# Infini-attention block: probabilities from a second, turned score product instead of transposes; row sums of the last head group on TensorE

## The chip, the cores and the metric

One core of a Trainium2 chip. The metric is the device time of one execution in microseconds (us), the median of several runs. The engines that matter here: TensorE (PE, with its weight loads PEld), VectorE (DVE), ScalarE (ACT), GpSimd (POOL), and SyncE (SP), whose queue issues nearly all DMAs.

## The reference

One pre-LayerNorm block on x of 1 x 2048 x 1024: an attention with a compressive memory, and then a channel MLP. There are H = 32 heads of width 32 and N = 4 segments of L = 512 rows. Cut to what matters:

```python
logits = einsum("bhqd,bhkd->bhqk", qs, ks) * scale + mask   # causal inside a segment, 512 x 512
p = softmax(logits)
a_dot = einsum("bhqk,bhkd->bhqd", p, vs)
pq = phi(qs)                                  # phi(t) = t + 1 if t > 0 else exp(t)
a_mem = (pq @ M) / (pq @ z + 1e-6)            # memory of the segments before
o = g * a_mem + (1 - g) * a_dot               # g = sigmoid(beta), one number a head
M, z = M + phi(ks).T @ vs, z + phi(ks).sum(0)
...
h = x + o @ wo
out = h + gelu(layernorm(h) @ w1 + b1) @ w2 + b2     # 1024 -> 3584 -> 1024
```

## The kernel before, in words

**Halves, groups, units.** The sequence is done in two halves of two segments. In each half the 32 heads are taken in eight groups `g` of four heads. A unit is one group in one segment: 2 x 8 x 2 = 32 units. After the 16 units of a half comes the product with `wo` (tile `pwo`); the MLP fills the rest of the span.

**Precision.** Each dense fp32 product is made of three fp32r products of high and low parts: `yh*wh`, `yl*wh`, `yh*wl`, the helper at L128, L129 and L130. A unit has 24 slots of such a triple (three projections `kps`, `qps`, `vps` of eight chunks of 128 rows), each matmul 128x512.

**Scores.** Query and key of a head are put on top of each other as high and low parts, so that one matmul with 96 rows makes the three partial products: `ks` has (high, low, high), `qs` (high, high, low). These stacks are written by DMA: `ks` goes through DRAM (`stack`, L410 and L412), `qs` for three heads from SBUF to SBUF (L407) and for one head through DRAM.

**The attention of a unit** runs one unit late, among the 24 slots of the next. `slot` has six steps for a head, and the table `HEAD` says at which step each operation of which pipeline stage is issued. For each head: four score matmuls `pqk` (L594, widths 128, 384, 256, 512, since a row block only needs the keys up to its diagonal); for each a DVE reduction (L595) that adds the mask, scales with minus, writes `pr` in SBUF and leaves the row minimum (minus the maximum) in `mx`; an ACT exponential (L603) with the row sum as its accumulator; ten PE transposes of 128x128 (`ppt`, L642, in groups of 4, 4 and 2); their copies to SBUF, one by DVE (L645, 512 wide) and two by ACT (L647, 512 and 256). After the four heads of a unit: the product with the values (`po`, L437, sixteen matmuls with 32 columns of weights, followed by the sixteen small `pmm` of the memory update); reciprocals of the sums (L610), times 1 - g on POOL (L613), transposed on PE (`pw`, L623), stored to `r_dram` (L626) and read back spread over 32 rows a head (L628); the scaling of `po` (L667) and the memory part (L670).

**Order.** PE keeps the program's order through the units. After the last unit's dense slots the order is free: there the scheduler mixes what is left of the attention with the matmuls of `pwo`. `TIMES` holds the slots of the unit's other operations (when keys and queries are evacuated, when a turned tile goes through `turn_dram` and back, when `o` is stored). SP issues its DMAs strictly in program order, and one that waits holds up those behind it.

**Banks.** PSUM: three banks for dense products, two `qk` for the scores, two `pt` for the transposes, one `av` for `po`. Weight casts `wh` of k and v are on ACT and that of q on DVE (L718), the low parts on POOL (L720).

## Time and profile before

| what | value |
|---|---|
| median of 3 runs | 2197.75 us (2196.99 to 2205.3) |
| the profiled execution | 2198.85 us |
| its span | 2197.1 us |
| granted TensorE clock over the span | 0.998 |
| PE busy | 2166.8 us (99%) |
| DVE busy | 1334.3 us (61%) |
| ACT busy | 1029.8 us (47%) |
| POOL busy | 740.2 us (34%) |
| DMA | 437.39 MB, mean 199 GB/s |

Busy times overlap one another. For PE the page models the ends of matmuls, and matmuls overlap in it, so a busy share of 99% says that PE is hardly ever empty, not that it works at its peak. What an instruction costs PE is read from the distance between two starts, in the timeline. The chain of waits follows the work that ended last back through whatever released it, and gives the share of the span by line.

### The profile page before, as it was taken

The numbers are of one execution on the slowest core, as the hardware profiler recorded it, in microseconds if no ns is written. First come the engines' busy times: TensorE is split into PE (matmuls) and PEld (weight loads), VectorE is DVE, ScalarE is ACT, GpSimd is POOL, SyncE is SP. The second block draws the span as 40 slices with busy tenths as digits, with TensorE's granted clock in tenths as the row PEclk, the third lists the DMA queues.
The fourth block names the chain that finished last, engine by engine and source line by source line (L and its number), as shares of the span: only waits on it lengthen the run. The fifth ranks groups of instructions, "written<-read, shape, count | busy, mean of one in ns | idle before, by whom it ended". The sixth has DMA issues, their size and how long they took to land.

```text
span 2197.1 us, 34393 instructions
## 1 busy us (share of the span) xinstructions
PE 2166.8 (99%) x11865; PEld 1758.3 (80%) x11865; DVE 1334.3 (61%) x2689; ACT 1029.8 (47%) x2219; POOL 740.2 (34%) x584
## 2 busy tenths in 40 slices
PE   8999999999999999999999999999999999999999
PEld 6788887868888887888888768888888788888887
DVE  6666665666745665666666656745666665576563
ACT  6566665653643445666666653543343222322321
POOL 4122221233434432122222233444445644155340
PEclk9999999999999999999999999999999999999999
DMA  7676666765575556666666755575659865576772
GB/s 229 187 198 183 192 195 196 201 200 201 173 215 163 172 160 192 184 193 188 196 191 185 202 178 197 159 211 157 182 177 375 290 229 192 180 248 219 243 240 91
DMA packets 400792, 437.39 MB, mean 199 GB/s; under 512 B 33102, under 2 KB 267114, under 8 KB 400618
## 3 DMA queue, kind: packets, MB, share of 16 engines
q1 hardware_dynamic: 337450, 398.48, 59.2%
q10 hardware_dynamic: 63168, 36.71, 5.6%
q8 instruction: 94, 1.54, 0.3%
q14 instruction: 80, 0.66, 0.1%
HBM read 287.41 MB, written 128.78 MB: 189 GB/s over the span
## 4 chain that ended last, share of the span: by engine, by line
PE 88%; DMA 3%; POOL 3%; ACT 2%; DVE 1%; issue 1%; SPq 1%; POOLq 0%; ACTq 0%
PE po L1376 21%; PE bps L980 10%; PE cps L980 7%; PE dps L980 7%; PE ppt L642 6%; PE pqk L594 4%; PE po L437 3%; PE qps L128 3%; PE kps L128 3%; PE vps L128 3%; PE kps L129 3%; PE kps L130 3%; PE qps L130 3%; PE qps L129 3%; PE vps L129 2%; PE vps L130 2%
## 5 line engine op out<-in xcount | busy, mean ns | idle before, releaser
L603 ACT ACTIVATE pr<-pr,mx 128x128 f32<-128x128 f32 (+3 forms) x512 | 287.0, 561 | 237.2 <-DVE mx L595 236.5
L595 DVE CUSTOM_DVE_ANT_0 pr<-pqk,mask 128x128 f32<-128x128 f32 (+3 forms) x512 | 241.3, 483 | 129.0 <-PE pqk L594 123.3
L642 PE MATMUL ppt<-ident,pr 128*128 128x128 f32 x1280 | 215.8, 273 | 5.1 <-ACT pr L603 2.3
L642 PEld LDWEIGHTS ppt<-ident,pr 128*128 128x128 f32 x1280 | 163.6, 140 | 54.5 <-DVE pt L645 3.7
L1386 DVE TENSOR_TENSOR c<-c,po 128x512 f32<-128x512 f32 x160 | 105.4, 683 | 138.9 <-PE po L1376 131.9
L594 PE MATMUL pqk<-ks,qs 96*128 96x128 f32 (+3 forms) x512 | 182.9, 359 | 2.9 <-DMA qs<-ql 1.8
L720 POOL TENSOR_TENSOR wl<-wr,wh 128x1024 fp32r<-128x1024 f32 x42 | 105.7, 2517 | 144.5 <-ACT wh L718 131.5
L647 ACT COPY pt<-ppt 128x512 f32<-128x512 f32 (+1 forms) x256 | 119.6, 468 | 55.9 <-PE po L437 38.9
L645 DVE COPY pt<-ppt 128x512 f32<-128x512 f32 x128 | 88.1, 689 | 70.3 <-PE ppt L642 59.3
L1376 PE MATMUL po<-w2h,zh 128*128 128x512 f32 x378 | 121.0, 390 | 1.4 <-ACT zh L1315 1.0
L594 PEld LDWEIGHTS pqk<-ks,qs 96*128 96x128 f32 x512 | 96.7, 189 | 21.8 <-issue 6.1
L980 PE MATMUL bps<-zh,sb 128*128 128x512 f32 x336 | 111.0, 391 | 0.0
L980 PE MATMUL bps<-zh,sa 128*128 128x512 f32 x336 | 110.8, 390 | 0.0
L128 PE MATMUL kps<-yh,wh 128*128 128x512 f32 (+1 forms) x264 | 110.0, 417 | 0.0
L1233 POOL TENSOR_TENSOR w2r<-w2r 128x512 f32<-128x512 f32 x54 | 84.0, 1565 | 71.2 <-DMA w2r<-in_B_w 68.6
L128 PE MATMUL qps<-yh,wh 128*128 128x512 f32 x256 | 107.4, 419 | 0.0
L128 PE MATMUL vps<-yh,wh 128*128 128x512 f32 x256 | 106.1, 414 | 0.0
L1376 PE MATMUL po<-w2h,hl 128*128 128x512 f32 x322 | 103.3, 390 | 0.2
L130 PE MATMUL kps<-yh,wl 128*128 128x512 f32 (+1 forms) x264 | 103.2, 391 | 0.0
L129 PE MATMUL kps<-yl,wh 128*128 128x512 f32 (+1 forms) x264 | 102.9, 390 | 0.1
L130 PE MATMUL vps<-yh,wl 128*128 128x512 f32 x256 | 100.8, 394 | 0.0
L130 PE MATMUL qps<-yh,wl 128*128 128x512 f32 x256 | 100.7, 394 | 0.0
(245 smaller groups left out, 5792.4 us busy)
## 6 DMA issues: line engine op xcount, KB each, us to landing
hr<-h_dram SPq DMA_DIRECT2D x112, 448.0 KB, 5.2
w2r<-in_B_w SPq DMA_DIRECT2D x122, 256.0 KB, 4.4
r<-in_B_w SPq DMA_DIRECT2D x56, 512.0 KB, 4.5
ks<-ks_dram SPq DMA_DIRECT2D x128, 192.0 KB, 3.5
h_dram<-ht ACTq DMA_DIRECT2D x84, 256.0 KB, 3.8
ks_dram<-kh SPq DMA_DIRECT2D x64, 256.0 KB, 2.7
wr<-in_A_wo SPq DMA_DIRECT2D x32, 512.0 KB, 4.6
wx<-in_B_w SPq DMA_DIRECT2D x56, 256.0 KB, 3.4
```

The lines of the kernel that those rows point to most:

```text
L128: nc.tensor.matmul(ps, ah, bh, start=first, stop=False)
L129: nc.tensor.matmul(ps, ah, bl, start=False, stop=False)
L130: acts["mm"] = nc.tensor.matmul(ps, al, bh, start=False, stop=last)
L594: nc.tensor.matmul(pqk[:, :n], u["qs"][j][:, i * P:(i + 1) * P], u["ks"][j][:, 0:n], start=True, stop=True)
L595: nc.vector.tensor_tensor_reduce(out=st["pr"][:, offs[i]:offs[i] + n], in0=pqk[:, :n], in1=mask[:, 512 - n:512], op0=ALU.add, op1=ALU.min, ...
L603: nc.scalar.activation(pi, pi, AF.Exp, bias=mx[:, i:i + 1], scale=-1.0, accum_out=mx[:, 4 + i:5 + i])
L642: nc.tensor.transpose(ppt[:, o:o + P], pr[:, offs[i] + jk * P:offs[i] + (jk + 1) * P], ident)
L647: nc.scalar.copy(pt, ppt[:, :w])
L720: nc.gpsimd.tensor_tensor(wl[:, c:c + WLC], wr[:, c:c + WLC], raw(wh)[:, c:c + WLC], op=ALU.subtract)
L980: nc.tensor.matmul(ps, x_[:, c, :], y_[:, c, :], start=first and c == 0 and n == 0, stop=last and c == 3 and n == 2, skip_group_check=True)
L1376: nc.tensor.matmul(ps, x_[:, k], y_[k], start=opens and k == 0 and i == 0, stop=closes and k == self.KP - 1 and i == 2, skip_group_check=True)
L1386: nc.vector.tensor_tensor(o, o, ps, op=ALU.subtract if name == "4" else ALU.add)
```

## The change

The probabilities are needed with the keys on the partitions, for the product with the values. Before, they were made with the queries on the partitions and turned on PE. Now a second score product makes them turned: `again` multiplies the stacks with their roles exchanged (`ks` as weights, `qs` as data; tile `psc`), and ACT's exponential of it is the tile that the value product reads. The row maximum has to be subtracted there along the columns, which is done in the product itself: the stacks have 98 rows, `ks` with 1.0 in the two more rows, and `qs` with minus the row maximum as a high and a low part.

```diff
-TIMES = dict(pk=10, kx=12, ks=11, qs=16, pq=16, omt=34, vx=24, pm=25, pmm=30, pmf=40, om=35, od=67, ...
+TIMES = dict(pk=12, kx=15, ks=9, kf=21, qs=17, qf=22, pq=18, omt=42, vx=24, pm=27, pmm=30, pmf=37, om=43, od=89, ...
+FOLLOW = dict(q=28.2, x=47.3, y=47.4, z=50.2, r=47.6, w=51.2, p=60.3, a=82.3, o=85.2)
+PACE = dict(q=(4.7,1.2), p=(4.0, 1.3))
...
+        def fetch(name, n, p):
+            nc.sync.dma_start(raw(stacks[name][n][0:96, 2 * p:2 * p + 2]),
+                              s_dram[name][n][64 * p:64 * p + 64].rearrange("(j r) b n -> (r b) j n", j=2))
...
+            for p in range(2):
+                at(T["kf"] + 7 * p, partial(stack_fetch, "ks", p))
+                at(T["qf"] + 6.5 * p, partial(stack_fetch, "qs", p))
...
+        def qk(u, j, i):
...
+            pqk = psum.tile([P, 512], F32, tag="qk", name="pqk", bufs=4)
...
+            nc.vector.tensor_tensor_reduce(out=pqk[:, :n], in0=pqk[:, :n], in1=mask[:, 512 - n:512], op0=ALU.add, op1=ALU.min,
+                                           scale=-1.0, scalar=3.0e38, accum_out=mx[:, k:k + 1])
+            if u["g"] < NG - 1:
+                nc.scalar.activation(pqk[:, :n], pqk[:, :n], AF.Exp, bias=mx[:, k:k + 1], scale=-1.0, accum_out=mx[:, 16 + k:17 + k])
...
+        def rows_in(u):
+            d = m_dram[u["md"]].rearrange("(a c k) r -> c k a r", a=4, c=2)
+            for c in range(2):
+                BQ.dma_start(raw(u["qs"][96 + c:97 + c]).rearrange("p j (i a r) -> p (j i) a r", i=4, a=4), d[c])
+
+        def again(u, j, n):
+            w = sum(P * (4 - jk) for jk in groups[n])
+            pt = ab.tile([P, w], F32, name=f"pt{n}", bufs=4)
+            ps = psum.tile([P, 512], F32, tag="qk", name="psc", bufs=4)
...
+                nc.tensor.matmul(ps[:, o:o + m], u["ks"][:, j, jk * P:(jk + 1) * P], u["qs"][:, j, P * jk:], start=True, stop=True)
...
+            nc.scalar.activation(pt, ps[:, :w], AF.Exp)
...
+            nc.gpsimd.affine_select(d, d, pattern=[[1, P]] if len(groups[n]) == 1 else [[0, 2], [1, P]],
+                                    compare_op=ALU.is_ge, fill=0.0, base=0, channel_multiplier=-1)
...
-            nc.vector.reciprocal(rs[:, 4 * j:4 * j + 4], st["mx"][:, 4:8])
...
+            if u["g"] == NG - 1:
+                den = psum.tile([P, 512], F32, tag="qk", name="den", bufs=4)
+                abreast([(den[32 * j:32 * j + 32, 0:P], ones, u["pt", 0][j][:, 0:P], True, True) for j in range(4)])
+                abreast([(den[32 * j:32 * j + 32, P:], ones, u["sm"][j], True, True) for j in range(4)])
+                nc.vector.reciprocal(u["w"], den)
```

What goes with it:

- **The first product stays**, with its reduction, but both now work in place in PSUM: its exponential is only for the row sums (`mx`), and nothing of it is copied out. Scores and second scores share one ring of four banks (`qk`), where there were two rings of two.
- **The maximum's way**: per unit a copy, a difference and a 32x32 block transpose of the 16 maxima of a row on DVE (`largest`), one store to `m_dram` (slot 47.4) and two loads of 1x64x32 into rows 96 and 97 of `qs` (slot 50.2). The second products begin at slot 60.3.
- **The mask** of the second product is an `affine_select` on POOL on each of the diagonal blocks after the exponential, three a head.
- **Stacks**: each unit stores three blocks of each stack to DRAM and fetches two heads at a time, 96x2x512. None of the stacks goes from SBUF to SBUF any more. The return of a turned tile from `turn_dram` (`back`) is issued three slots after its store (`HOP`).
- **The last group of a half** (`g == 7`, two units a half, four in all) makes no row sums on ACT. DVE adds the turned probabilities into `sm` (three additions a head), eight fp32 matmuls with ones make the sums already spread as `po` is (`den`), a reciprocal of 128x512 on DVE inverts them, and one more instruction (L721 of the new kernel) scales `po`. The way over `pw` and `r_dram` is left out there.
- **Scale and casts**: the scale is folded into the evacuation of the queries. The weight casts of k and v go from ACT to DVE, so that all three are there.
- **Time**: the attention of a unit now reaches from slot 28 to slot 85 after its unit's start, so that it spans two following units; `HEAD` and `slot` are gone, and every operation has its slot in `FOLLOW` or `LAST_FOLLOW` and its distance between heads in `PACE` or `LAST_PACE`.

The line numbers of the new kernel differ from those of the profile before. On PE, in the `vps` slots of a unit in the middle of a half, the program before had this for one head (`yh`, `yl`: the input's parts; `wh`, `wl`: the weights'):

```order
L594 MATMUL pqk<-ks,qs 128x128
L128 MATMUL vps<-yh_204,wh 128x512
L129 MATMUL vps<-yl_205,wh 128x512
L130 MATMUL vps<-yh_204,wl 128x512
L642 MATMUL ppt<-ident,pr 128x128 x4
L594 MATMUL pqk<-ks,qs 128x384
```

In the changed program the same place, the `vps` slots of a unit, reads:

```order
L664 MATMUL psc<-qs_374,ks_372 128x512
L632 MATMUL pqk<-ks_373,qs_375 128x256
L135 MATMUL vps<-yh_439,wh 128x512
L136 MATMUL vps<-yl_440,wh 128x512
L137 MATMUL vps<-yh_439,wl 128x512
L664 MATMUL psc<-qs_374,ks_372 128x384
L664 MATMUL psc<-qs_374,ks_372 128x128
L632 MATMUL pqk<-ks_373,qs_375 128x512
```

Where a group of four transposes stood beside a score matmul, one or two matmuls of the second product of the unit before (`ks_372`, `qs_374`) stand beside a score matmul of the current one (`ks_373`, `qs_375`).

On SP, around the point where the inverse sums of a unit go out to `r_dram`, before (`qs_dram`, `ks_dram`: stacks; `turn_dram`: a turned tile; `wr`: a weight):

```order
L412 DMA qs<-qs_dram_166 96x512
L374 DMA sch<-turn_dram_159 32x4x128 x4
L626 DMA r_dram_161<-sch 16x128
L410 DMA ks_dram_163<-kh 128x512
L410 DMA ks_dram_163<-kl 128x512
L410 DMA ks_dram_163<-kh 128x512
L628 DMA sch<-r_dram_161 32x512 x4
```

The same point in the changed program:

```order
L648 DMA m_dram_169<-mt 128x32
L381 DMA turn_dram_160<-sch 128x512
L697 DMA r_dram_163<-sch 16x128
L420 DMA ks_373<-ks_dram_166 96x2x512
L653 DMA qs_374<-m_dram_169 1x64x32 x2
L386 DMA sch<-turn_dram_160 32x4x128 x4
L699 DMA sch<-r_dram_163 32x512 x4
L420 DMA qs_375<-qs_dram_168 96x2x512
```

The fetch of the second half of the next unit's query stack (the last row) stands behind the store and the reload of the inverse sums, behind the two loads of the maxima and behind the return of a turned tile. Before, the query stack had been issued ahead of the store.

On DVE, after the dense slots of a half have ended, with the first of the two last units at its end (`sm`, `den`: the sums of the last group):

```order
L678 TENSOR_TENSOR sm<-sm,pt_5560 128x256
L547 TENSOR_TENSOR MZ<-pmm,MZ 128x128
L634 ISA pqk,mx<-pqk,mask 128x128
L634 ISA mx 128x1
L711 RECIPROCAL scl<-den 128x512
L634 ISA pqk,mx<-pqk,mask 128x384
```

Before, the scaling of `po` in that place stood with a copy of a transposed tile and with no reciprocal of that size:

```order
L610 RECIPROCAL rs<-mx 128x4
L645 COPY pt_6249<-ppt 128x512
L529 TENSOR_TENSOR MZ<-pmm,MZ 128x128
L667 TENSOR_TENSOR scl<-po,scl 128x512
L104 TENSOR_TENSOR ol_5550<-scl,oh_5549 128x512
```

The wide reciprocal and the additions of `sm` have come in between the reductions of the very last unit and the scaling of `po`.

More of the change, by code (lines that the diff above doesn't have):

```diff
@@ L96, in build @@
     s_dram = {n: [dram.tile([P, 3, 512], F32, name=f"{n}_dram{k}") for k in range(2)] for n in ("ks", "qs")}
+    m_dram = [dram.tile([P, 32], F32, name=f"m_dram{k}") for k in range(2)]
     acts = {}
@@ L372, in turned, with back @@
             TQ.dma_start(d, mid)
+            return d
+        def back(d, to):
             for c in range(4):
@@ L545, in memory_turn @@
                     one_small()
-                turned(v["om"], u["omt"], tmp("omx"))
+                d = turned(v["om"], tmp("omx"))
+                at(T["om"] + HOP, lambda: back(d, u["omt"]))
             if g < NG - 1:
@@ L1045, in c1 @@
                 if j < HP:
-                    ps = self.banks[j] = bank("cps", ("qk", "pt")[j % 2], 2)
+                    ps = self.banks[j] = bank("cps", "qk", 4)
                     h, l, _ = left[j - 2]
@@ L1128, in pair @@
             self.made(j + 1, "S2", "S1")
-            dps = bank("dps", "pt", 2)
+            dps = bank("dps", "qk", 4)
             if j < HP - 1:
```

265 lines of the change are left out of this document (130 added, 135 removed).

## The prediction

> **What bounds the kernel now.** First the page's busy times and its chain of waits:
>
> ```profile
> PE 2166.8 (99%) x11865; PEld 1758.3 (80%) x11865; DVE 1334.3 (61%) x2689; ACT 1029.8 (47%) x2219; POOL 740.2 (34%) x584
> PE 88%; DMA 3%; POOL 3%; ACT 2%; DVE 1%; issue 1%; SPq 1%; POOLq 0%; ACTq 0%
> by line: PE po L1376 21.2%; PE bps L980 10.3%; PE cps L980 7.0%; PE dps L980 6.8%; PE ppt L642 5.8%; PE pqk L594 3.6%; PE po L437 2.9%; PE qps L128 2.7%; PE kps L128 2.6%; PE vps L128 2.6%; PE kps L129 2.5%; PE kps L130 2.5%; PE qps L130 2.
> ```
>
> The end is set by PE for 88% of the span. The transposes `ppt` hold 5.8% of it, 0.058 x 2197.1 = 127.4 us, or 127.4 / 128 = 1.0 us for each of the 128 heads in segments; the four score matmuls hold 3.6%, 79.1 us, 0.62 us a head. Then four windows of 27 us: two with dense slots and attention in the two halves, and the two tails, where the last units meet the product with `wo`. Columns after the window: span, then the busy time of PE, PEld, DVE, ACT, POOL, then clock, DMA share and GB/s.
>
> ```profile
> 404.00:431.00 27.00, 27.00 (x198) 21.63 (x196) 16.63 (x52) 16.52 (x47) 1.88 (x5) 1.00 0.65 191
> 1037.00:1064.00 27.00, 27.00 (x170) 21.60 (x169) 17.65 (x56) 17.00 (x48) 7.00 (x5) 1.00 0.52 152
> 458.00:485.00 27.00, 24.75 (x144) 18.69 (x143) 17.24 (x34) 13.53 (x33) 8.10 (x7) 1.00 0.61 201
> 1289.00:1316.00 27.00, 25.86 (x134) 17.98 (x133) 14.80 (x24) 10.71 (x23) 11.86 (x9) 1.00 0.59 177
> ```
>
> In the first two PE never idles at clock 1.00, and DVE and ACT have some 10 us free: there a microsecond off PE's queue is a microsecond off the time, as long as nobody makes PE wait. The tails are looser already: PE is empty for 27.00 - 24.75 = 2.25 and 27.00 - 25.86 = 1.14 us. Last, PE's timeline over one head (start, duration; durations overlap, so I use starts):
>
> ```profile
> 405.83 0.23 PE L594 MATMUL pqk<-ks,qs 96*128 96x128 f32 x1
> ...
> 406.63 0.60 PE L642 MATMUL ppt<-ident,pr 128*128 128x128 f32 x4
> 406.98 0.44 PE L594 MATMUL pqk<-ks,qs 96*128 96x384 f32 x1
> ...
> 407.95 0.28 PE L594 MATMUL pqk<-ks,qs 96*128 96x256 f32 x1
> ...
> 408.77 0.60 PE L642 MATMUL ppt<-ident,pr 128*128 128x128 f32 x4
> 409.12 0.48 PE L594 MATMUL pqk<-ks,qs 96*128 96x512 f32 x1
> ...
> 410.14 0.38 PE L642 MATMUL ppt<-ident,pr 128*128 128x128 f32 x2
> 410.27 0.48 PE L128 MATMUL vps<-yh,wh 128*128 128x512 f32 x1
> 410.59 0.40 PE L129 MATMUL vps<-yl,wh 128*128 128x512 f32 x1
> ...
> 411.75 0.22 PE L594 MATMUL pqk<-ks,qs 96*128 96x128 f32 x1
> ```
>
> From 410.59 to 411.75 five dense matmuls start: 0.232 us each. The head's 18 of them make 4.18 of its 5.92 us; 1.74 us are attention. The transposes take 0.35 + 0.35 + 0.13 = 0.83 directly, and the matmul behind each group comes about 0.09 late (410.27 to 410.59 is 0.32, not 0.232): 1.10 us. The four score matmuls keep the rest, 0.64. Both agree with the chain.
>
> **Term 1: transposes out, a second product in.** Gone are 1.0 to 1.10 us a head. Four matmuls of the same widths as `pqk` come in; no row shows them with 98 rows and two fetched heads side by side, so I price them as the first product, 0.62 to 0.64. The difference is 127.4 - 79.1 = 48 us by the chain and (1.10 - 0.64) x 128 = 59 us by the timeline. I take -53.
>
> On this the Trainium skill (TensorE: Matmul & The Clock Gate, Back-to-back issue gap) gives sustained spacings of about 81 ns at 128 columns and 131 ns at 512. By them, interpolating, ten transposes against 512 + 384 + 128 + 256 columns would save an estimated 0.39 us a head, 49 us; but the trace's dense matmul takes 232 ns, so its figures are not those of this stream, and I stay with the rows.
>
> **Term 2: row sums on PE.** In the four last units the `den` matmuls stream 128 + 384 columns a head, with the form of `po`, which streams 1280:
>
> ```profile
> 427.18 2.36 PE L437 MATMUL po<-pt,sch 128*32 128x512 f32 x32
> 429.35 0.48 PE L437 MATMUL pmm<-sch,scl 128*32 128x32 f32 x32
> 429.76 0.50 PE L594 MATMUL pqk<-ks,qs 96*128 96x512 f32 x1
> ```
>
> `po` takes 429.35 - 427.18 = 2.17 us, so `den` takes 512/1280 of it, 0.87, and four units 3.5 us: +3.5.
>
> **Term 3: new waits among the dense slots** (28 units outside the last groups). Two candidates.
>
> (i) The second half of the next unit's queries. Behind `pw` SP issues, in order: the store to `r_dram`, half a key stack, two loads of maxima, the return of a turned tile, the reload of the inverse sums, and only then this fetch. The rows of SP (issue time of a group) and of landing:
>
> ```profile
> 352.82 2.98 SPq L412 DMA_DIRECT2D ks<-ks_dram  x4
> 368.40 1.95 SPq L374 DMA_DIRECT2D sch<-turn_dram  x4
> 370.45 0.72 SPq L626 DMA_DIRECT2D r_dram<-sch  x1
> 372.69 1.80 SPq L628 DMA_DIRECT2D sch<-r_dram  x4
> ks<-ks_dram SPq DMA_DIRECT2D x128, 192.0 KB, 3.5
> qs<-qs_dram SPq DMA_DIRECT2D x32, 192.0 KB, 4.9
> 481.05 0.27 PE L623 MATMUL pw<-ident,rs 128*16 128x128 f32 x1
> L624 ACT COPY sch<-pw 16x128 f32<-16x128 f32 x7 | 1.8, 251 | 0.0
> ```
>
> `pw` and its copy with their handing over: about 0.7. Issues: 0.72 + 2.98/4 + 1.0 (two small loads, at 0.5 by the same rows) + 1.95 + 1.80 = 6.2. Landing 4.9. Together 11.8 us behind `pw`. PE gets from `pw` (slot 51.2) to the first score of head 2 (28.2 + 2 x 4.7 + 24 = 61.6) by ten triples, 10 x 3 x 0.232 = 6.96, two heads of scores 1.28, the first second products 0.52, and `po` with `pmm` 429.76 - 427.18 = 2.58: 11.3 us. So PE is about 0.5 us late; not at all if the fetch lands in 3.5, and 2.9 if its 384 KB cost another half of 4.9 (rival B).
>
> The skill (DMA: Bandwidth & Descriptors, Anatomy of one DMA) fits about 2.0 us plus bytes over 436e3 for a DMA of the gpsimd path, an estimated 2.9 us for 384 KB: no wait, and a sum 6 us lower. The trace's 4.9 for half the bytes speaks against it.
>
> (ii) The ring. A score bank is held through DVE and, new, through ACT's exponential:
>
> ```profile
> L595 DVE CUSTOM_DVE_ANT_0 pr<-pqk,mask 128x512 f32<-128x512 f32 x52 | 35.9, 690 | 22.0 <-PE pqk L594 20.4
> L595 DVE DVE_READ_ACCUMULATOR2_ANT mx<- 128x1 f32 x207 | 17.3, 83 | 0.0
> L603 ACT ACTIVATE pr<-pr,mx 128x512 f32<-128x512 f32 x52 | 37.7, 725 | 22.0 <-DVE mx L595 21.8
> L603 ACT ACTIVATION_READ_ACCUMULATOR pr<-pr,mx 128x1 f32 x208 | 39.3, 189 | 0.0
> L603 ACT ACTIVATE pr<-pr,mx 128x256 f32<-128x256 f32 x52 | 26.0, 501 | 0.0
> L647 ACT COPY pt<-ppt 128x512 f32<-128x512 f32 x52 | 29.9, 574 | 15.7 <-PE po L437 15.1
> ```
>
> A wide one: 0.69 + 0.08 + 0.73 + 0.19 plus handing over, about 2 us, against four banks. Where both products run, in some ten slots, ACT has for each head four exponentials with their read-outs, (0.725 + 0.501)/2 + 0.189 = 0.80 each on average, and three of the second product, 1.95 (1.5 if it reads PSUM as fast as the copy does): 4.7 to 5.2 us. A head takes 4 to 4.7 slots there, each 0.70 with some 0.3 of attention: 4.0 to 4.7 us. So a bank can come late for two or three heads, I say by 0.2 to 0.3 us a unit.
>
> While PE waits for the one the ring drains, so the two don't add in full: 0.45 us a unit, 28 x 0.45 = +12.6 (0 to 36, the upper end being 1.3 us a unit).
>
> **Off the path.** ACT gets a second exponential, at most 4 x (0.725 + 0.725 + 0.501) = 7.8 us a unit, and loses copies of 4 x (0.574 + 0.357) = 3.7 and about one weight cast of 1.05: from 16.5 to at most 19.6 of some 26 us, hidden by PE's dense slots. DVE loses four copies of 0.690, and gets that cast. POOL gets twelve selects a unit:
>
> ```profile
> L349 POOL TENSOR_SCALAR_AFFINE_SELECT mask<-mask 128x128 f32<-128x128 f32 x2 | 0.6, 296 | 0.1
> L507 DVE RECIPROCAL rg<-rg 128x8 f32<-128x8 f32 x48 | 9.2, 196 | 0.7
> L80 DVE RECIPROCAL gate<-bb 128x32 f32<-128x32 f32 x1 | 0.3, 333 | 0.0
> L670 POOL TENSOR_TENSOR sch<-sch,omt 128x512 f32<-128x512 f32 x14 | 18.2, 1299 | 63.2 <-DVE sch L667 57.8 <-DMA ks_dram<-kh 5.4
> ```
>
> At 0.30 for one block and somewhat more for two, about 4.4 us; the last second product is at about slot 75 and `po` at 82.3, seven triples or 4.9 us, which cover the last head's 1.1 us and more that may stand ahead of them in POOL's queue. Without that cover it would cost some 1 to 3 us a unit. The queries' scale is folded into instructions that were there: nothing.
>
> **Term 4: the two tails.** Without dense slots between them, PE's bunch of the last units has second products, scores, `po` and `den`: about 7.4 us, while DVE has thirteen reductions (three heads of 2.27 and one of 0.37, 7.2) and three heads' additions of `sm` (at about 1.25): 10.9. That is 3.4 us of waiting. Behind `den` comes the reciprocal of 128x512. The rows of 8 and 32 elements differ by 137 ns over 24 elements, 5.7 ns each, so 512 take about 3.0 us; behind it in DVE's queue are three reductions (1.9), then the scaling (0.69), POOL's addition (1.30) and a split on ACT (0.6), 7.5 us until `wo` has the last chunk, against some 5 us of other products: 2.5 more. The very last unit I put at 1.5. That makes 7.4 us a half against the 2.25 and 1.14 seen before: 14.8 - 3.4 = 11.4. Since the order is free there and some of DVE's work can lie ahead, I take +8 (0 to 14).
>
> **Sum.** 2198.85 - 53 + 3.5 + 12.6 + 8 = 2170.0 for a profiled execution. The one of before was 1.1 above the median, so **2169**. By the terms' ends: 2198.85 - 59 + 3.5 = 2143 to 2198.85 - 48 + 3.5 + 36 + 14 = 2204.
>
> **Rivals.**
>
> A. The waits eat the saving: ring and fetch together cost about 1.5 us a unit. For it: ACT is full for ten slots and holds the ring. Against: DVE and ACT each have 10 us free in a unit to catch up. 2198.85 - 53 + 3.5 + 28 x 1.5 + 8 = 2199, median 2198. Chance 0.13.
>
> B. Slower: the fetch of 384 KB lands in 4.9 x 1.5 = 7.3 us, so that the second half of the queries is 2.9 us late in every unit. 2198.85 - 53 + 3.5 + 28 x 2.9 + 8 = 2238, median 2237. It breaks even at (53 - 3.5 - 8) / 28 = 1.48 us a unit and is clearly slower from 1.48 + 11/28 = 1.87. For it: SP's order puts the fetch last, and DMA is at 0.65 in that window. Against: landing is not in proportion to bytes (page: 64 KB in 2.0, 512 KB in 4.7).
>
> ```profile
> qs<-qh SPq DMA_DIRECT2D x192, 64.0 KB, 2.0
> wr<-in_A_wk SPq DMA_DIRECT2D x16, 512.0 KB, 4.7
> ```
>
> Chance 0.10.
>
> C. Nothing is saved on PE: the ten transposes stream 1280 columns, and so does the second product. If PE's time went by columns alone, term 1 were 0 and the time 2198.85 + 3.5 + 12.6 + 8 = 2223, median 2222. Against it: the rows above, 1.10 against 0.64 for the same columns. The skill's isolated gap (TensorE: Matmul & The Clock Gate, Back-to-back issue gap: columns over 2.4 plus 2.5 ns) would have it so, within 2 us. Chance 0.04.
>
> **How the numbers follow.** Forecast 0.73, A 0.13, B 0.10, C 0.04. A measurement of this kernel tells about 0.5%, 11 us, from no change: faster is below 2187, slower above 2209. The forecast is faster, A the same, B and C slower: 0.73, 0.13, 0.14. The range goes from near the lower end of the terms, 2145, to 2202, which takes in A and leaves out B and C.
>
> **What would show it.** Right: no `ppt` in the chain, the second product at about 3.6% of it like `pqk`; from one `po` to the next, in the middle of a half, 4 x (1.10 - 0.64) - 0.45 = 1.4 us less than before; PE's waits at `pqk` of head 2 for the DMA of `qs` near 0.5 us and at score banks below that; idle PE of 5 to 8 us in each tail with DVE's reciprocal as releaser. Wrong: waits of over 1.5 us a unit at the fetch (B) or for ACT at `psc` and `pqk` (A), a second product that costs as much as the transposes (C), or POOL's selects named as what `po` waits for, the cover that I counted on.

## The result and the profile after

The changed kernel takes 2222.09 us (median of 4 runs, 2220.32 to 2223.31) against 2198.83 us (4 runs) for the one before: slower by a ratio of 1.010, interval 1.0078 to 1.0122. Forecast were 2169 us and a range from 2145 to 2202. Its profiled execution has a span of 2221.6 us, 24.5 more than before, and a mean granted clock of 0.992 instead of 0.998.

The same page rows as before, busy times and the chain by line:

```profile
PE 2151.2 (97%) x11157; PEld 1712.9 (77%) x11157; DVE 1333.8 (60%) x2638; ACT 1026.4 (46%) x2187; POOL 866.8 (39%) x968
PE 85%; DMA 4%; DVE 4%; issue 2%; POOL 2%; ACT 2%; SPq 1%; POOLq 0%; DVEq 0%; ACTq 0%
by line: PE po L1411 23.1%; PE bps L1015 10.4%; PE cps L1015 7.1%; PE dps L1015 7.0%; PE po L446 3.3%; PE pqk L632 3.1%; PE psc L664 2.9%; PE qps L135 2.4%; PE kps L135 2.3%; PE vps L135 2.3%; PE kps L136 2.2%; PE vps L136 2.2%; PE vps L137
```

`ppt` is gone and `psc` holds 2.9%, less than `pqk` held (3.6%): the trade on PE itself is as good as forecast. But PE's share of the chain has fallen, and DMA, DVE and "issue" have risen. Where, is seen when the span is cut at the same points of the program: the first and the last `vps` of a half, the last `pwo`, the first `kps` of the second half. The windows view of the kernel before, by stage: opening, units, tail with `wo`, MLP, then the second half's units, tail and the rest (columns: span, busy PE, PEld, DVE, ACT, POOL, clock, DMA share, GB/s):

```profile
0.00:29.60 29.60, 20.18 (x116) 17.74 (x117) 21.10 (x43) 16.86 (x24) 17.59 (x36) 1.00 0.76 241
29.60:442.60 413.00, 410.70 (x2952) 330.51 (x2951) 254.41 (x796) 253.58 (x714) 85.91 (x94) 1.00 0.69 195
442.60:558.80 116.20, 111.79 (x591) 86.36 (x590) 68.04 (x123) 49.30 (x92) 39.42 (x40) 1.00 0.57 187
558.80:833.20 274.40, 274.40 (x1243) 227.12 (x1242) 162.46 (x214) 126.20 (x193) 115.52 (x92) 1.00 0.59 177
833.20:1267.20 434.00, 429.72 (x2851) 345.81 (x2850) 268.44 (x837) 260.67 (x718) 93.39 (x88) 1.00 0.68 195
1267.20:1386.00 118.80, 114.36 (x560) 86.33 (x559) 69.85 (x123) 50.86 (x93) 39.61 (x39) 0.99 0.52 168
1386.00:2197.00 811.00, 805.68 (x3562) 664.46 (x3560) 490.00 (x556) 272.37 (x390) 348.76 (x197) 1.00 0.66 215
```

The same of the changed kernel:

```profile
0.00:39.90 39.90, 21.59 (x116) 18.68 (x117) 23.05 (x48) 18.83 (x26) 22.26 (x42) 0.91 0.60 191
39.90:429.20 389.30, 382.80 (x2553) 302.69 (x2552) 238.71 (x748) 254.09 (x717) 138.92 (x253) 1.00 0.77 230
429.20:565.00 135.80, 125.44 (x637) 90.63 (x636) 81.87 (x139) 46.28 (x69) 47.39 (x66) 0.97 0.49 160
565.00:844.00 279.00, 279.00 (x1243) 226.92 (x1242) 162.13 (x214) 126.34 (x193) 116.61 (x93) 1.00 0.58 174
844.00:1260.80 416.80, 402.54 (x2451) 315.79 (x2450) 251.89 (x795) 261.81 (x726) 148.68 (x253) 1.00 0.76 225
1260.80:1408.30 147.50, 130.68 (x605) 93.50 (x604) 84.44 (x140) 46.16 (x69) 46.98 (x67) 0.93 0.42 136
1408.30:2221.60 813.30, 809.14 (x3562) 664.73 (x3560) 491.72 (x556) 272.89 (x390) 345.96 (x197) 1.00 0.66 215
```

Row by row: the opening +10.3 us, the units -23.7 and -17.2, the tails +19.6 and +28.7, the MLP stages +4.6 and +2.3. The sum is 24.6, the 24.5 up to rounding. So the units gave 40.9 us, and it was lost in three places, of which the prediction had priced one, and that at 8 us. That terms 1 and 3 together said -53 + 12.6 = -40.4 is partly luck: the units' stages do not hold all of the heads, as the section on the prediction works out. Three things in the rows: in the tails PE is empty for 10.4 and 16.8 us (span less busy) against 4.4 and 4.4; the clock there is 0.97 and 0.93; and the MLP of the first half, with the same 1243 matmuls, no idle time and clock 1.00, is 4.6 us longer.

### The profile page after: what moved, and what is told of

It reads as the page before. It is cut to its first block, busy times and chain, and to the rows that moved or that the text cites. A ratio compares the mean times of both kernels' runs of the same rounds, so it can differ in the third digit from the quotient of the medians.

```text
span 2221.6 us, 33312 instructions
## 1 busy us (share of the span) xinstructions
PE 2151.2 (97%) x11157; PEld 1712.9 (77%) x11157; DVE 1333.8 (60%) x2638; ACT 1026.4 (46%) x2187; POOL 866.8 (39%) x968
## 3 DMA queue, kind: packets, MB, share of 16 engines
q1 hardware_dynamic: 351466, 417.31, 60.3%
## 4 chain that ended last, share of the span: by engine, by line
PE 85%; DMA 4%; DVE 4%; issue 2%; POOL 2%; ACT 2%; SPq 1%; POOLq 0%; DVEq 0%; ACTq 0%
PE po L1411 23%; PE bps L1015 10%; PE cps L1015 7%; PE dps L1015 7%; PE po L446 3%; PE pqk L632 3%; PE psc L664 3%; PE qps L135 2%; PE kps L135 2%; PE vps L135 2%; PE kps L136 2%; PE vps L136 2%; PE vps L137 2%; PE kps L137 2%; PE qps L136 2%; PE qps L137 2%
## 5 line engine op out<-in xcount | busy, mean ns | idle before, releaser
L634 DVE CUSTOM_DVE_ANT_0 pqk<-pqk,mask 128x128 f32<-128x128 f32 (+3 forms) x512 | 252.4, 498 | 245.0 <-PE pqk L632 231.5
L637 ACT ACTIVATE pqk<-pqk,mx 128x128 f32<-128x128 f32 x448 | 225.8, 504 | 198.9 <-DVE mx L634 192.5
L668 POOL TENSOR_SCALAR_AFFINE_SELECT pt<-pt 128x128 f32<-128x128 f32 (+1 forms) x384 | 136.3, 361 | 285.0 <-ACT pt L666 282.2
L666 ACT ACTIVATE pt<-psc 128x512 f32<-128x512 f32 (+1 forms) x384 | 197.2, 528 | 96.0 <-PE psc L664 91.5
L632 PE MATMUL pqk<-ks,qs 96*128 96x128 f32 (+3 forms) x512 | 173.3, 341 | 13.0 <-DMA qs<-qs_dram 8.9
L664 PE MATMUL psc<-qs,ks 98*128 98x512 f32 (+3 forms) x512 | 139.5, 319 | 10.7 <-ACT pqk L637 8.7
L664 PEld LDWEIGHTS psc<-qs,ks 98*128 98x128 f32 x512 | 95.2, 189 | 41.7 <-ACT pqk L637 12.9
L756 POOL TENSOR_TENSOR wl<-wr,wh 128x1024 fp32r<-128x1024 f32 x42 | 100.6, 2395 | 56.6 <-PE pqk L632 39.4
L136 PE MATMUL qps<-yl,wh 128*128 128x512 f32 x256 | 101.6, 397 | 0.0
## 6 DMA issues: line engine op xcount, KB each, us to landing
ks<-ks_dram SPq DMA_DIRECT2D x64, 384.0 KB, 4.0
qs<-qs_dram SPq DMA_DIRECT2D x64, 384.0 KB, 4.5
```

Source lines behind the costliest of these rows:

```text
L136: nc.tensor.matmul(ps, ah, bl, start=False, stop=False)
L632: nc.tensor.matmul(pqk[:, :n], u["qs"][0:96, j, i * P:(i + 1) * P], u["ks"][0:96, j, 0:n], start=True, stop=True)
L634: nc.vector.tensor_tensor_reduce(out=pqk[:, :n], in0=pqk[:, :n], in1=mask[:, 512 - n:512], op0=ALU.add, op1=ALU.min, scale=-1.0, scalar=3. ...
L637: nc.scalar.activation(pqk[:, :n], pqk[:, :n], AF.Exp, bias=mx[:, k:k + 1], scale=-1.0, accum_out=mx[:, 16 + k:17 + k])
L664: nc.tensor.matmul(ps[:, o:o + m], u["ks"][:, j, jk * P:(jk + 1) * P], u["qs"][:, j, P * jk:], start=True, stop=True)
L666: nc.scalar.activation(pt, ps[:, :w], AF.Exp)
```

## The experiments

My theory after the two traces: three causes in three places, which add. In the tails, the way of the maxima (first product of a whole unit, reduction, DVE, a store to DRAM and two loads back), which now stands in front of the second product of the last units. In the opening, four loads of beta in elements of 4 bytes and two memsets. In the MLP, the tiles' addresses. The rivals were: for the tails the new sums (`den` and its reciprocal), too little ready `wo` work, or the `wo` weights; for the MLP the banks, which the change joined into one ring of four.

The runs stood on several chips, so each is given by its ratio to the kernel before on its own chip, with its 95% interval, and compared with the changed kernel's 1.010 (1.0078 to 1.0122); 0.1% is 2.2 us. Stages of other runs are cut at the same points as above.

### The addresses

The built programs give each tile's place in SBUF. Before, the weights, scratch and stacks start at 480 modulo 512 bytes, and so do the inputs and the MLP's tiles at the other end. The change adds 224 bytes of constants (`ones`, longer `gate` and `bb`), and everything behind them starts at 192. Run a480 pads to 480 again, a224 to 224, and b192 gives the kernel before the changed kernel's place:

```diff
-    hsel = const.tile([P, 76], F32, name="hsel")[:, 0:4]
+    hsel = const.tile([P, 148], F32, name="hsel")[:, 0:4]
```

(84 columns in a224; 132 in b192, there in the kernel before.)

> Only a pad of 288 bytes in the pool of constants, so that the tiles behind it (weights, stacks, scratch) start again at 480 modulo 512 as in the kernel before. Theory (address): the MLP's matmuls, 0.2334 us apart in cps in the changed kernel against 0.2268 before, go back to 0.2268; the two MLP stages give back 4.6 + 2.3 us and the units and the product with wo some 3 to 6 more: 10 to 13 us less than the changed kernel, about 2210. Rival (the banks: cps and dps now share the ring of four): the spacing stays at 0.2334 and the time at 2222.

> The kernel before with a pad of 224 bytes in the same place, so that its weights and scratch start at 192 modulo 512 as in the changed kernel. Address theory: cps goes from 0.2268 to 0.2334 us and the time from 2198 to 2208 to 2211. Rival (banks or the new instructions): no change, 2198.

> The changed kernel with a pad of 32 bytes, so that weights and scratch start at 224 modulo 512, which is 32 modulo 64 as at 480, but not 480. If an odd multiple of 32 bytes is what the fast matmuls have in common: cps at 0.2268 us as before. If it is the place modulo 512 (the same as that of the right-hand pools): still 0.233.

The chain's rows for 36 matmuls of `cps` in the first half (start, length, count), of before, changed, a480, b192 and a224 in this order:

```profile
576.55 8.20 PE cps L980 x36
```

```profile
571.74 8.41 PE cps L1015 x36
```

```profile
572.75 8.20 PE cps L1015 x36
```

```profile
568.17 8.41 PE cps L980 x36
```

```profile
593.91 8.20 PE cps L1015 x36
```

The spacing, 8.20/36 = 0.228 or 8.41/36 = 0.234 us, goes with the address and not with the banks: a480 and a224 have the changed kernel's ring of four. The first half's MLP, 274.4 us before and 279.0 after, took 274.3 in a480 and a224 and 278.9 in b192. In time, b192 is slower than its kernel before by 1.0029 (1.0016 to 1.0041), 6 us, and a480 stands at 1.0076 (1.0061 to 1.0090), some 5 us better than the change, though the intervals overlap. Both are about half of what was expected; a224 was executed once. So the stage rows show the effect, and the times of the whole only its size of 5 to 6 us. It shows in the MLP and not in the units: those of b192 take 412.2 and 432.0 us, no more than the 413.0 and 434.0 before. The fast places, 480 and 224, are both 32 modulo 64 (and both 224 modulo 256, which these three places can't tell apart); the slow one, 192, is 0 modulo 64, beside operands that were at 32. Whether 0 for all operands would be fast was not tried.

### The opening

SP's issues in the opening (start, length of the issue), first of the kernel before, then of the changed one, and two memsets of its POOL:

```profile
5.06 4.22 SPq L258 DMA_DIRECT2D bb<-in_A_beta  x1
...
15.63 0.38 SPq L246 DMA_DIRECT2D wr<-in_A_wv  x1
```

```profile
6.68 3.66 SPq L265 DMA_DIRECT2D bb<-in_A_beta  x1
10.38 2.23 SPq L267 DMA_DIRECT2D bb<-in_A_beta  x4
...
19.76 1.08 SPq L253 DMA_DIRECT2D wr<-in_A_wv  x1
```

```profile
6.02 1.80 POOL L411 MEMSET ks<- 2x2048 f32 x1
8.52 1.80 POOL L411 MEMSET ks<- 2x2048 f32 x1
```

The first load of beta, 128 rows of 32 numbers, is in both kernels (4.22 and 3.66 us); new are the four small ones, which hold SP for 2.23 us. The v weights are issued at 19.76 us instead of 15.63. The memsets stand on POOL between the small operations of the first LayerNorm. Run open takes gate's column from the gate that is there, and puts the memsets behind the opening's POOL work:

```diff
-        for h in range(4):
-            nc.sync.dma_start(bb[32 * h:32 * h + 32, H:], bass.AP(tensor=beta.tensor, offset=beta.offset + h, ap=[[0, DH], [4, NG]]))
...
+        for h in range(4):
+            nc.vector.tensor_copy(gate[32 * h:32 * h + 32, 1, H + NG - 1:H + NG], gate[32 * h:32 * h + 32, 1, H - 4 + h:H - 3 + h])
...
-            nc.gpsimd.memset(raw(st[96:98]), 1.0)
+            op = nc.gpsimd.memset(raw(st[96:98]), 1.0)
+            if half == 0:
+                behind(op)
```

> The changed kernel without its four extra loads of beta in elements of 4 bytes (the values are copied on DVE from the gate that is there) and with the two memsets of the stacks' rows of ones held back on POOL until the opening is over. Theory (the opening's 10.3 us are these two): first v product at 30 to 32 instead of 39.9 us, the time 8 to 10 us lower, about 2213. Rival (the start is hidden by later waits, or DMA by the other loads is what is late): first v product later than 36 us, time within 4 us of 2222.

Without the four loads the v weights are issued at 15.48 us again. The opening shrank from 39.9 to 34.7 us, not to 30: the memsets, now at 22 to 26 us, hold up the low part of the v weights on POOL instead. The ratio is 1.0088 (1.0073 to 1.0104), which by itself can't be told from the change. In the run combo below, with the memsets behind the whole first unit, the opening is 31.3 us long, 8.6 less than in the changed kernel. Its length varies, though: in the other runs that leave the opening as it is, it is 36.7 to 39.3 us. So the two edits give some 5 to 9 us.

### The tails: what is waited for

In the second half's tail of the changed kernel, three windows of 4 us, and PE's longest wait there:

```profile
1301.00:1305.00 4.00, 0.77 (x6) 0.44 (x3) 3.87 (x4) 0.83 (x2) 1.26 (x1) 1.00 0.32 107
1305.00:1309.00 4.00, 0.32 (x1) 0.32 (x2) 3.52 (x10) 0.99 (x2) 1.26 (x1) 0.55 0.07 25
1309.00:1313.00 4.00, 4.00 (x12) 3.07 (x12) 3.90 (x6) 0.15 (x1) 0.00 (x0) 0.60 0.19 37
```

```profile
PE pwo L135 <- ACT oh L110: 6.9, 1, 6.9
```

and DVE in that time:

```profile
1301.13 3.36 DVE L711 RECIPROCAL scl<-den 128x512 f32<-128x512 f32 x1 [2.52 <-PE den L446]
1304.40 0.54 DVE L634 CUSTOM_DVE_ANT_0 pqk<-pqk,mask 128x384 f32<-128x384 f32 x1
...
1305.89 0.75 DVE L721 SCALAR_TENSOR_TENSOR scl<-po,gate,scl 128x512 f32<-128x512 f32 x1
1306.55 0.17 DVE L642 CAST top<-mx 128x16 fp32r<-128x16 f32 x1
...
1308.05 0.21 DVE L644 STREAM_TRANSPOSE mt<-top 128x32 f32<-128x32 f32 x1
```

PE is empty for 6.9 us while DVE's one queue does it all: the reciprocal of the first of the last two units, the last three reductions of the second, the scaling of the first, and only then the maxima of the second, which go out to DRAM at 1308 us. By its own row PE waits here for the first unit's output (`oh`), and the work that could have filled the gap, the second products of the last unit, has to wait for the maxima. They come at 1325 us; the last of them starts 69.6 us after the tail has begun. In the other groups the loads of the maxima stand at slot 50.2 and the second product at 60.3; in the last group these are slots 46.1 and 50.3.

In the two windows of 4 us with the gap's end and behind it the clock is at 0.55 and 0.60. The Trainium skill (TensorE: Matmul & The Clock Gate, What's actually happening) says that the gate gives half the pulses after an idle window of about 3.4 us; the rows of this gap agree with it. In the first half's tail, though, the clock fell without such a gap:

```profile
448.00:452.00 4.00, 2.51 (x8) 1.27 (x8) 4.00 (x15) 1.80 (x5) 1.00 (x3) 1.00 0.30 41
452.00:456.00 4.00, 3.92 (x15) 1.55 (x19) 2.78 (x12) 0.77 (x2) 2.17 (x4) 0.57 0.46 136
```

In the first of these windows PE was busy for 2.51 of 4 us, and its longest single wait was 0.63 us. The waits of that tail are many small ones, none over 2.0 us; 6.1 us of the 10.4 are for the high and low parts of the `wo` weights, whose casts stand in the queues of ACT, DVE and POOL.

Run nomax takes the first product, the reduction and the maxima out of the last group; nochain leaves them in and only lets the second product go without them (96 rows), and doesn't load them either; nochain_sp as nochain, with the loads kept. All three leave out the subtraction of the maximum in the last group's second product:

```diff
         def qk(u, j, i):
+            if u["g"] == NG - 1:
+                return
```

(nomax; the same in largest, rows_out and rows_in; nochain has it in rows_in alone, nochain_sp nowhere), and in all three

```diff
-                nc.tensor.matmul(ps[:, o:o + m], u["ks"][:, j, jk * P:(jk + 1) * P], u["qs"][:, j, P * jk:], start=True, stop=True)
+                k = 96 if u["g"] == NG - 1 else 98
+                nc.tensor.matmul(ps[:, o:o + m], u["ks"][0:k, j, jk * P:(jk + 1) * P], u["qs"][0:k, j, P * jk:], start=True, stop=True)
```

> The changed kernel with the last group's four units without first score product, row maxima and their subtraction (left out; the sums of the last group are made from the turned probabilities anyway). Theory (the tails are long because each of the last two units needs its whole first product, DVE's reductions and the maxima's way before its second product can start): 10 us of PE work go, and with them at least another 10 us of waiting and of low clock in the two tails: 2222 to about 2200. Rival (the tails wait for the wo weights and their buffers): only PE's work goes, some 8 to 10 us, about 2213.

> The changed kernel, in which the last group's second products use 96 rows and do not wait for the maxima (the subtraction of the maximum is left out there; first products, reductions and maxima are still made, and nothing of them is used). It tells the wait for the maxima from the work. Wait theory: of the 44 us that leaving out the whole first product brought, over half come back, 2185 to 2200. Work theory (PE's 10 us and DVE's 9 us a unit, which hold the ring of banks): 2208 to 2222.

> The changed kernel, in which the last group's second products use 96 rows and so do not wait for the maxima (their subtraction is left out there), while all the loads of the maxima stay in SP's queue as they are. If PE's wait and the place in the order that comes of it are the price: as the run that left out the loads too, 2188 to 2196. If SP's queue behind the two loads is: 2210 to 2222.

Ratios: nomax 0.9895 (0.9875 to 0.9915), nochain 0.9955 (0.9940 to 0.9969), nochain_sp 1.0003 (0.9991 to 1.0015). Against 1.010 that is 45, 32 and 21 us less. So of nomax's 45 us 32 are the wait and 13 the work (PE's share of it, 16 heads of 0.63, is 10). Of the 32, 21 go when PE's product alone needn't wait, and 11 more when the two loads leave SP's queue; nochain_sp's time lies between the two ranges that were expected. Its stages, against nochain's, put 8.5 us of this into the second tail (135.1) and 4.5 into the last stage (818.1), and none into the first tail (122.4); which issue of SP is held up there was not looked at. The two tails of nochain:

```profile
427.00:550.80 123.80, 118.77 (x638) 90.08 (x637) 80.41 (x139) 46.55 (x69) 48.92 (x66) 0.99 0.53 175
1247.30:1373.90 126.60, 120.33 (x606) 87.74 (x605) 82.97 (x140) 46.84 (x69) 51.17 (x67) 1.00 0.51 158
```

Against 135.8 and 147.5 they are 12.0 and 20.9 us shorter, 32.9 together, with as many matmuls but for one in each, and the clock is back at 0.99 and 1.00. About half of it is waiting and half the slow clock: PE is empty for 11.3 us instead of 27.2, and busy for 239.1 us instead of 256.1 with the same work. The last second product starts 45.9 us after the second tail has begun, not 69.6, and PE's longest single wait in the two tails is 1.9 us. The rest over the kernel before, 250.4 - (116.2 + 118.8) = 15.4 us, is mostly work: PE is busy 7.0 and 6.0 us more than in the tails of before, 13.0, and empty 2.4 us more. The windows of nochain's two tails again, for the line that issues `po`, `pmm` and `den`, and for that line in the kernel before:

```profile
427.00:550.80 123.80, 13.10 (x160) 4.93 (x160) 0.99 0.53 175
1247.30:1373.90 126.60, 15.23 (x128) 4.12 (x128) 1.00 0.51 158
```

```profile
442.60:558.80 116.20, 5.79 (x96) 2.27 (x96) 1.00 0.57 187
1267.20:1386.00 118.80, 7.61 (x64) 1.66 (x64) 0.99 0.52 168
```

That line has 64 matmuls more in each tail: 32 are the two `den` (16 each in the trace), and 32 the `po` of one more unit, which ran under dense slots before; together 7.3 and 7.6 us. The second products cost the tails hardly more, although there are more of them: 36 matmuls (nine heads) keep PE busy for 9.86 and 10.34 us, and the 52 transposes of before (5.2 heads) did so for 10.06 and 9.20 us.

### The tails: the sums

Run oldsums gives the last group the other groups' sums (accumulators on ACT, `pw`, `r_dram`), without `den`, `sm` and the wide reciprocal; each of the six conditions on the last group is taken out like this one:

```diff
-            if u["g"] == NG - 1:
+            if False:
                 den = psum.tile([P, 512], F32, tag="qk", name="den", bufs=4)
```

> The changed kernel with the other half of the change undone: the last group makes its row sums as the other groups do (ACT's accumulators, pw, store and reload of the inverse sums), without den, sm and the wide reciprocal. Theory (the tails are long because the first product, the maxima and the second product of both last units stand in them): not faster, 2218 to 2240, as the way over DRAM is added again. Rival (the sums on PE with their 3.4 us reciprocal are what costs): at least 10 us less, below 2212.

The ratio is 1.0043 (1.0026 to 1.0060), 12.5 us less than the change: the rival holds, and my theory, that the run would not be faster, falls. The sums on PE, part of the change, cost more than the way over DRAM that they save. Its tails, 16.6 us shorter together, while its units are 6.4 us longer:

```profile
432.40:563.80 131.40, 123.47 (x606) 90.03 (x605) 62.51 (x114) 54.35 (x102) 46.87 (x70) 0.99 0.51 167
1260.70:1396.00 135.30, 126.89 (x574) 91.59 (x573) 64.95 (x113) 55.14 (x105) 49.56 (x69) 0.95 0.48 150
```

DVE is busy 62.5 and 65.0 us there instead of 81.9 and 84.4: the additions and the reciprocals (3.36 us each) stood in the one queue that also makes the maxima.

### The tails: what did not help

wo3 starts three `wo` blocks ahead of the chunk that waits for the last group, instead of two; wo3_12 also spreads the remaining attention (`RA, RH` 1.2 and 18); wocast puts the casts of the `wo` weights' high parts on DVE and their low parts on POOL; direct has the maxima turned by PE and sends them from SBUF to SBUF:

```diff
-        for t in (0, 1):
+        for t in (0, 1, 2):
             yield from block(0, t, range(NG - 2))
-        for t in (0, 1):
+        for t in (0, 1, 2):
             yield from block(0, t, range(NG - 2, NG))
...
-        split(None, wr, h, l, "scalar", "gpsimd" if k % 2 else "vector")
+        split(None, wr, h, l, "vector", "gpsimd")
...
+                nc.tensor.transpose(pm[0:32, 0:P], raw(top).rearrange("p c k -> p (c k)"), ident)
+                u["mt"] = ab.tile([32, P], F32, name="mu", bufs=1)
+                nc.vector.tensor_copy(u["mt"], pm[0:32, 0:P])
...
+                    BQ.dma_start(raw(u["qs"][96 + c:97 + c]).rearrange("p j (i q) -> p (j i) q", i=4), u["mt"][16 * c:16 * c + 16, :])
```

> The changed kernel with three blocks of the product with wo (instead of two) started on the chunks that are ready, ahead of the chunk that waits for the last group: 18 triples, 12.5 us of PE, instead of 12, to cover the tail. Theory (PE lacks ready work while the first of the last units finishes): 5 to 10 us less, 2212 to 2217. Rival (the tail is held by the order of the scratch buffers and by SP's queue): within 3 us of 2222.

> As the run with three blocks started, and the attention's remaining slots are spread at 1.2 a triple over the first 18 triples instead of 1.8 over 14 (with two blocks the program order needs 1.8). Theory (the bunch of attention without other work between, where PE waits for DVE and ACT, is the price): another 5 to 15 us less than the run with three blocks, 2200 to 2210. Rival: the last unit ends later and nothing is gained, 2215 or more.

> The changed kernel with the casts of wo's high parts on DVE instead of ACT (their low parts then all on POOL). Theory (in the tail the casts stand in ACT's queue behind the last unit's exponentials, which wait 10.7 us for a second product that comes late; wo's loads and its matmuls at 512 to 530 us then wait for the casts): 5 to 12 us less, 2210 to 2217. Rival (the buffers are what is late, or DVE's own queue is as full): within 3 us of 2222 or slower.

> The changed kernel, in which the last group's maxima are turned by a PE transpose and go from SBUF straight into rows 96 and 97 (two transfers with runs of 512 bytes) instead of through DRAM (a store, then two loads with runs of 128 bytes). Theory (the maxima's way is the wait in the tails, 33 us of them): the way is 2 to 3 us shorter for each of four units, so 5 to 15 us less, 2207 to 2217. Rival (the wait is in the place that the second product got in the order, not in the transfer's own length): within 4 us of 2222.

Ratios: wo3 1.0110 (1.0089 to 1.0131), wo3_12 1.0138 (1.0119 to 1.0157), wocast 1.0179 (1.0166 to 1.0193), direct 1.0078 (1.0064 to 1.0091). More ready `wo` work is no cure, and spreading the attention as well makes it no better. My theory on wocast, drawn from these rows of the changed kernel, was wrong:

```profile
483.17 4.61 ACT L666 ACTIVATE pt<-psc 128x512 f32<-128x512 f32 x10 [10.70 <-PE psc L664]
487.62 1.08 ACT L110 CAST wh<-wr 128x1024 fp32r<-128x1024 f32 x1
```

The casts do stand behind ACT's wait of 10.7 us, but on DVE and POOL they cost 17 us more: in the changed kernel's first tail DVE is busy for 81.9 us and ACT for 46.3. direct gains 5 us, the low end of what was expected, and its interval overlaps that of the change. What it gained does not lie where the theory had it: its two tails take 138.1 and 144.3 us, 282.4 together against 283.3. So in this kernel the length of the transfer is not what the tails wait for.

### Put together

combo is a480, the opening (memsets behind the first unit) and oldsums in one; combo_direct adds direct, cd_z then moves the maxima's transfers from slot 46.1 to 42.8, and with them the way of the inverse sums (`w`) from 46.2 to 44.2; nochain_c is combo with the edits of nochain, so it leaves out the subtraction in the last group's second products, which its row sums still contain. The edit of cd_z:

```diff
-LAST_FOLLOW = dict(q=28.2, x=42.3, y=42.4, z=46.1, r=42.6, w=46.2, p=50.3, a=63.3, o=66.2)
+LAST_FOLLOW = dict(q=28.2, x=42.3, y=42.4, z=42.8, r=42.9, w=44.2, p=50.3, a=63.3, o=66.2)
```

> The changed kernel with everything put right that the runs showed beside the maxima: addresses back at 480 modulo 512 (5 to 7 us), no extra loads of beta and the memsets behind the first unit (8), the last group's sums on ACT as in the other groups (12). If the three add up: 25 to 27 us less than 2222, 2195 to 2198, level with the kernel before. If the tails hide one another's parts: 2203 to 2210.

> As the run with all three put right, and the last group's maxima go straight from SBUF to SBUF. If the way of the maxima is still what the tails wait for: another 5 to 15 us less, 2182 to 2192, faster than the kernel before. If not: level with the run without it.

> The version with addresses, opening and sums put right and the last group's maxima sent from SBUF to SBUF, with these transfers issued 3.3 slots earlier in the program (slot 42.8 instead of 46.1, ahead of the store of the inverse sums). If the maxima's place in SP's queue is what the tails wait for: 4 to 10 us less than without, 2182 to 2188. If not: the same, 2190 to 2194.

> The version with addresses, opening and sums put right, and the last group's second products without the wait for the maxima (subtraction and loads left out there). If the wait for the maxima is a part of its own: 15 to 30 us below that version, 2165 to 2180. If the sums put right had already taken the same slack: within 8 us of it, 2186 to 2194.

combo stands at 0.9968 (0.9955 to 0.9981), 29 us below the change and 7 below the kernel before: a480's 5 and oldsums' 12.5, with the 5 to 9 by the rows of the opening, make 23 to 26, so the three corrections do not hide one another. combo_direct is at 0.9963 (0.9952 to 0.9975), not to be told from combo, although its two tails are 8.0 us shorter together (126.9 and 130.6 us against 131.2 and 134.3), since its units are 4.2 us longer. cd_z is at 0.9931 (0.9913 to 0.9948): some 15 us faster than the kernel before (by the medians, 2187.88 against 2200.65, 13 us), the fastest run that leaves nothing out. As it moves two things, it doesn't tell which of them gave the 7 us over combo_direct. nochain_c is at 0.9886 (0.9873 to 0.9898), 18 us below combo. So the wait for the maxima is still there, but only 18 of its 32 us. The other 14 went with the three corrections, most likely with the reciprocals and additions that stood ahead of the maxima on DVE; no run takes these apart.

In cd_z's first half the units take 397.0 us, longer than the changed kernel's 389.3; the opening (32.0) and the tail (126.9) are 7.9 and 8.9 us shorter. In its second tail the last second product starts 49.0 us after the beginning.

## Why the prediction was wrong

**Term 1** (transposes against a second product, -53) held. PE's timeline of the changed kernel over a head's second product (start, length; the lengths overlap, so the starts count):

```profile
208.54 0.39 PE L664 MATMUL psc<-qs,ks 98*128 98x512 f32 x1
208.77 0.39 PE L632 MATMUL pqk<-ks,qs 96*128 96x512 f32 x1
...
209.70 0.40 PE L664 MATMUL psc<-qs,ks 98*128 98x384 f32 x2
209.94 0.27 PE L632 MATMUL pqk<-ks,qs 96*128 96x128 f32 x1
...
210.97 0.28 PE L664 MATMUL psc<-qs,ks 98*128 98x256 f32 x1
211.09 0.40 PE L135 MATMUL qps<-yh,wh 128*128 128x512 f32 x1
```

The next matmul starts 0.23, 0.24 (for 384 and 128 columns) and 0.12 us later, 0.59 us in all and with no late start, against the 0.62 to 0.64 taken. Rival C, no saving on PE, is out. The chain puts it at 0.029 x 2221.6 / 128 = 0.50.

**Term 2** (`den`, +3.5) counted PE's own part alone. In nochain's tails the rows of `den` keep PE busy for 3.4 and 4.4 us, 7.8 together, an upper bound, since they overlap `po`. What the new sums cost in all, with DVE's additions and reciprocals, is the 12.5 us of oldsums.

**Term 3** (waits among the dense slots, +12.6) was right in size: PE's empty time in the two units' stages grew from 2.3 and 4.3 to 6.5 and 14.3 us, +14.2, and by both kinds that were named. The longest in the second half:

```profile
PE psc L664 <- ACT pqk L637: 8.7, 13, 1.0
PE pqk L632 <- DMA qs<-qs_dram: 4.2, 3, 1.7
```

Rival A, 1.5 us a unit, is out: 14.2 / 28 is 0.5. Rival B is out: the fetch of 384 KB landed in 4.5 us (median), not 7.3, as the row `qs<-qs_dram SPq DMA_DIRECT2D x64, 384.0 KB, 4.5` of its page has it. By this part alone the kernel would have been faster, and the cover of POOL's selects held too: no wait of `po` for them is among PE's waits in the two stages. By the counts of the tails the units held 64 - 5.2 = 58.8 heads of transposes a half before, and hold 64 - 9 = 55 second products now: 2 x (58.8 x 1.0 to 1.10 - 55 x 0.59) = 53 to 64 us, with the two `po` that left (2.2 each) 57 to 69, less 14.2 of waits 43 to 55. Seen were 40.9; where the 2 to 14 us between went I did not find. It is not the addresses: a480's units take 389.7 and 415.8 us, the changed kernel's 389.3 and 416.8.

**Term 4** (the tails, +8) is the step that failed; they took 48.3. By the rows above these are 18.3 us more of empty PE, 17.0 us more of PE's time for the same work (what nochain gives back of it; the granted clock is 0.97 and 0.93 there, against 0.99 and 1.00), and 13.0 us more of PE work.

It counted each engine's own work and took 8 of an excess of 11.4 "since the order is free there". But the order is not free: the second product of the last units is bound to the whole first product, through DVE's queue, a store and two loads. Leaving out that bond gives 33 us of the two tails back. Term 4 had the reciprocal right (3.0 forecast, 3.36 measured), saw the three reductions behind it, and put the way of the first unit's output to `wo` at 7.5 us, of which "some 5 us of other products" would cover a part. It did not see that the last unit's maxima wait behind the same queue, so that the second products that might have been this cover come only later: in the second half PE was empty for 6.9 us where 2.5 were forecast. In place of its "idle PE of 5 to 8 us in each tail" there were 10.4 and 16.8, and the low clock was in no term. Of the 13 us of PE work, term 2 had 3.5 for `den`; the `po` that the longer pipeline leaves for the end was counted nowhere.

**Not priced at all** were the opening (10.3 us) and the MLP stages (6.9). The prediction read neither the loads of beta and the memsets, which are in the diff, nor the move of every tile behind one new and two longer constants, which no row of the profile of before could show.

## What to carry to other kernels

A trade that pays in the steady part is paid for where the pipeline drains: count how much of each unit is left when the cover ends, and write out the one chain that the last unit goes through, queue by queue. Cut the span at the same points of both programs before looking for causes; three of the seven rows here had nothing to do with the idea of the change. And look at setup loads, memsets and the addresses behind a constant that got longer, since they can eat a good part of what an idea brings: here 17 of 41 us. Two side effects put right, and the new sums taken back, gave 29 us.

## What was not expected of the hardware

In the MLP the same matmul of 512 columns starts every 0.228 us or every 0.234 us, by the place in SBUF of the tiles behind the constants. With 480 modulo 512 bytes it was fast and with 192 slow, in both kernels, and with 224, tried in the changed one, it was fast.

Small loads hold SP for long: one of 128 rows of 32 numbers for 3.66 us (4.22 in the kernel before), and four of 32 x 8 single numbers for 2.23 us together.

PE's gap of 6.9 us in the second tail went on costing after it had ended: the granted clock was 0.55 and 0.60 in the two windows of 4 us around and behind it. And no such gap was needed: in the first tail it was 0.57 in the 4 us behind a window in which PE was busy for 2.51 of 4 us, with no wait over 0.63 us.
